# Gathered rows turned by a 16-bit DMA transpose instead of by TensorE

## The chip, the cores and the metric

One core of one Trainium2 chip runs the whole program. The metric is the device time of one execution in microseconds (us), as the median of several runs. The core has five engines with a queue of instructions each: TensorE (PE; its weight loads are listed apart as PEld), VectorE (DVE), ScalarE (ACT), GpSimd (POOL) and SyncE (SP). SP only issues DMAs; GpSimd issues the indirect ones.

## The reference

A gated linear attention (batch 4, 8 heads, 768 positions, head size 48) keeps a 48 x 48 state per head; its output is viewed as 3072 tokens of 384 numbers. A noisy gate picks 2 of 8 experts for each token; each expert is a two-layer network (384 to 1024 to 384, relu). A dense two-layer network follows (384 to 2048 to 384, leaky). All numbers are float32.

```python
state = alpha_t[:, None] * state + outer(k_t, v_t);  y_t = q_t @ state
noisy = x @ w_gate + log1p(exp(x @ w_noise)) * noise       # top 2 of 8, softmax of the two
out[token] += weight * (relu(x[token] @ w1[e]) @ w2[e])
h = out @ w_in;  result = maximum(0.01 * h, h) @ w_out
```

## The kernel before, in words

**Stages.** The attention works through 24 units of 128 tokens. Each unit ends with a turn of its output to rows of tokens (`turn_y`), a copy out of PSUM by ScalarE (`copy_x`, L1026) and a store to the DRAM buffer `x_d` (L1033). Routing gives each choice of a token a slot in `idx_d` (scatter by GpSimd, L1142). Then 16 expert groups follow, two per expert: group kind 0 has 384 slots (3 blocks of 128 rows), kind 1 has 480 (4 blocks of 120). The first two groups, experts 0 and 1 with kind 0, take rows of the first 2048 tokens alone and so can begin early. Eight dense groups of 384 tokens end the program.

**Input of a group.** For each block `gather1` (L511) fetches rows of `x_d` by an indirect DMA into the tile `xg` (a ring of six). `turn` (L521 to L529) turns the block with three 128-column transposes on TensorE into the PSUM tile `pA` (a ring of two). `turned_hi` (L533, ScalarE) copies the result rounded into `xh`, and `turned_lo` (L538, VectorE) stores the rest into `xl`; there are two sets of `xh` and `xl`. For a dense group `gather2` (L731) fetches the two experts' rows of each token, and `combine` (L738 on ScalarE, L740 on VectorE) adds them by weight; the result is turned in the same way.

**Products.** `gemm1` (L669) does nine matmuls for 128 hidden columns, three pieces of 128 rows with three products of halves of precision, into `ph` (two PSUM buffers). `hidden` makes `hh` (L686, ScalarE) and `hl` (L693, VectorE) out of it, in dense groups by way of `hc` (L679 to L696). `gemm2` (L708) does three matmuls per block and step into `py`, two steps behind `gemm1`. A group has 8 such steps, a dense group 16. `rows_out` and `rows_stored` (L725) bring the result to `y_d` or to the output.

**Order.** A planner written in Python (`Planner`) places every step: it is given the engine (p, a, v, g, s, or a choice such as vg), an estimated duration, an extra latency for DMAs (`lat`), the steps that it depends on, the rings that it takes and a due time. It always takes the step that can start earliest by its own estimates, and among equals the one due first. The result is a fixed order on each engine; the chip then waits by semaphores. The SP queue carries, in that order, loads of attention inputs, weights (`fetch`, L444, L447), stores of `x_d` and `y_d`, and the spills and reloads of the dense weights (L482, L487).

```python
w = add("p", 0.34, lambda j=j: turn(key, j), own + AUX.get((key, j), []), ...,
        due=tm[0] - 7 + 0.8 * j if phase == 2 else 1e9)
hi = add("a", 0.5, lambda j=j: turned_hi(key, j), ...)
lo = add("v", 0.57, lambda j=j: turned_lo(key, j), [hi], ...)
```

Of the kernel before, what the change touches and what calls it, by code (L numbers as in the profile page):

```python
# [7 lines left out]
FT = mybir.dt.float32  # L8
# [3 lines left out]
U32 = mybir.dt.uint32  # L12
AF = mybir.ActivationFunctionType
# [15 lines left out]
F64B = 2  # L29
XGB = 6  # L30
# [293 lines left out]
def tile_kernel(  # L324
# [39 lines left out]
    x_d = dram.tile([N, Dm], FT, name="x_d")  # L364
# [130 lines left out]
    def slots_of(t, g):  # L495
        return t[1 + E * OFF[g]:1 + E * (OFF[g] + GR[g]), :].rearrange("(p j e) d -> p j e d", e=E, j=len(GB[g]))

    def rows_of(t, e, g, j):

        return slots_of(t, g)[:, j, e, :]  # L500
# [3 lines left out]
    def load_idx(i, g):  # L504
        src = slots_of(idx_d, g).rearrange("p j e o -> p (j e o)")
        nc.sync.dma_start(idx_sb[i][:GB[g][0][1]].rearrange("p j e -> p (j e)"), src.bitcast(U32))

    def gather1(e, g, j, rows, i):
        o, n = GB[g][j]
        xg = xgp.tile([128, Dm], FT, name="xg")  # L510
# [8 lines left out]
    XT, XP = {}, {}  # L519

    def turn(key, j):  # L521
        if j == 0:
            pool = pools["M" if len(XT) % 2 else "E"]
            XT[key] = [pool.tile([128, KD, GMAX], FR, name=nm, bufs=1) for nm in ("xh", "xl")]
        o, n = blocks(key)[j]
        src = xg_t.pop(key + (j,))
# [4 lines left out]
    def turned_hi(key, j):  # L531
        o, n = blocks(key)[j]
        nc.scalar.activation(XT[key][0][:, :, o:o + n], XP[key, j][:, :, :n], AF.Copy)  # L533
# [44 lines left out]
    def build_experts(t0, R, stored, scat, early_in, ready_at, totals, acc_done, begun):  # L578
# [7 lines left out]
        def rows_in(e, g):  # L586
            for j in range(len(GB[g])):
                if g == 0 and e < EARLY:
                    deps, rows = [early_in] + stored[:EARLY_TILES * NG], EARLY_TILES * TT
                else:  # L590
                    deps, rows = [late_in[1 - g]] + stored, N
                GX["a", e, g, j] = add("g", 1.29, lambda j=j, rows=rows: gather1(e, g, j, rows, 2 if rows < N else g), deps, takes=[R["xg"]],
                                       lat=2.0)

        def turned(key, phase):
            done = []
            for j, (o, n) in enumerate(blocks(key)):
                own = [XO[key]] if j else []
                w = add("p", 0.34, lambda j=j: turn(key, j), own + AUX.get((key, j), []),
                        use=[(GX[key + (j,)], R["xg"])] + [(x, R["XT"]) for x in own],  # L600
                        takes=[R["pA"]] + ([] if j else [R["XT"]]), phase=phase, due=tm[0] - 7 + 0.8 * j if phase == 2 else 1e9)
                if not j:
                    XO[key] = w
                hi = add("a", 0.5, lambda j=j: turned_hi(key, j), use=[(w, R["pA"]), (XO[key], R["XT"])], phase=phase)
                lo = add("v", 0.57, lambda j=j: turned_lo(key, j), [hi], use=[(w, R["pA"]), (XO[key], R["XT"])], phase=phase)
                done += [hi, lo]
            return done
# [126 lines left out]
        def combine(g, j, kk):  # L734
            c = g * (GROUP2 // 128) + j
            ya = YG["b", g, j, 0]
            if kk == 0:
                nc.scalar.activation(ya, ya, AF.Copy, scale=wts[:, c, 0:1])  # L738
            else:
                nc.vector.scalar_tensor_tensor(ya, YG["b", g, j, 1], wts[:, c, 1:2], ya, op0=OP.mult, op1=OP.add)  # L740
                xg_t["b", 0, g, j] = ya
# [5 lines left out]
        def group_in(gi):  # L747
# [3 lines left out]
            else:  # L751
                for j in range(len(blocks(key))):
# [6 lines left out]
                    GX[key + (j,)] = ga  # L759
                    AUX[key, j] = [cb]  # L760
                    ga.holders[R["xg"]].append(cb)
# [69 lines left out]
    with ExitStack() as actx:  # L831
# [14 lines left out]
            scr=1, pend=PB, pA=2, xg=XGB, XT=2, W=NA + NB, w1s=2, w2s=2, ph=2, hh=4, hl=4, py=4, ys=3, hc=2, f64=F64B, f64o=2).items()}  # L846
# [6 lines left out]
        def build_unit(u):  # L853
# [178 lines left out]
            cx = add("a", 0.5, copy_x, use=[(ty, R["pA"])], takes=[R["x"]])  # L1032
            xo = add("s", 0.07, lambda: nc.sync.dma_start(x_d[u * C:(u + 1) * C, :], d["x"].rearrange("p h s d -> p (h s d)")),  # L1033
# [177 lines left out]
    with tc.If(fv > 0):  # L1211
        general(tc, dict(q=q, k=k, v=v, alpha=alpha), identf, hm, desc, wgn_l, noise, x_d, w1, w2, w_in, w_out, out)
# [219 lines left out]
```

## Time and profile before

| what | value |
|---|---|
| median of 3 runs | 1102.26 us (1102.2 to 1102.77) |
| span of the profiled execution | 1088.6 us |
| median less that span | 13.7 us |
| mean granted TensorE clock | 0.987 |
| instructions in the span | 17738 |
| DMA traffic | 127.37 MB, 117 GB/s in the mean |

The span runs from the first to the last instruction of one execution. The profile gives no total for that execution beside its span, so the span is set against the median of the runs. Each engine's busy time is a sum over its instructions; matmuls are pipelined, so that the records of neighbours overlap, and a granted clock of 1.0 is 2.4 GHz. In a timeline a line gives the start, the time, the engine, the source line, the operation with its result and inputs, and how many were merged, and in brackets the idle time before it and who ended it.

### The profile page before, as it was taken

What the parts mean: (1) busy time and instruction counts of PE and PEld (TensorE: products, weight loads), DVE (VectorE), ACT (ScalarE), POOL (GpSimd) and SP (SyncE); (2) the same over time, 40 slices, a digit from 0 to 9 for tenths busy, and PEclk for the clock granted to TensorE, in tenths of its full rate; (3) what the DMA queues carried; (4) which work ended last, traced back from release to release, by engine and by line L of the source; (5) the groups of instructions that cost most, each with busy time, mean ns of one, the idle gap of its engine ahead of it and who ended that gap; (6) DMA issues with size and microseconds to landing.
All of it is one profiled execution on the core that took longest, in us unless ns stands there. A gap on an engine that the chain in (4) does not pass through costs nothing.

```text
span 1088.6 us, 17738 instructions
## 1 busy us (share of the span) xinstructions
PE 1056.3 (97%) x6600; PEld 989.9 (91%) x6600; DVE 585.1 (54%) x1199; ACT 392.2 (36%) x835; POOL 325.3 (30%) x386
## 2 busy tenths in 40 slices
PE   7989897999999999999999999999999999999997
PEld 5756763999999999999999999999999999999997
DVE  8797964522545564654565334555554545454543
ACT  5656554322444453534453333231222222222211
POOL 4456676531123343544262131310110102010000
PEclk9998998999999999999999999999999999999999
DMA  9989813133544464655476665320101111000000
GB/s 253 287 177 224 162 56 122 26 92 108 157 120 162 145 211 134 215 162 162 156 230 213 193 202 169 116 66 9 58 19 48 30 37 34 32 23 23 1 22 26
DMA packets 76967, 127.37 MB, mean 117 GB/s; under 512 B 10407, under 2 KB 54311, under 8 KB 76871
## 3 DMA queue, kind: packets, MB, share of 16 engines
q1 hardware_dynamic: 68679, 106.05, 33.0%
q0 software_dynamic: 8192, 20.09, 6.6%
q8 instruction: 54, 0.88, 0.4%
q14 instruction: 42, 0.34, 0.1%
HBM read 93.42 MB, written 32.69 MB: 116 GB/s over the span
## 4 chain that ended last, share of the span: by engine, by line
PE 82%; issue 0%; DVE 0%; ACT 0%; DMA 0%; ACTq 0%
PE py L708 40%; PE ph L669 39%; PE pA L529 2%; DVE w1lB L457 0%; ACT ys L718 0%; DVE w2lB L457 0%; ACT w1hB L453 0%; DVE xl L538 0%; PE pA L557 0%; DVE g_um L201 0%; DVE g_u L193 0%; DMA x_d<-x 0%; ACTq L453 0%; PE pA L1113 0%; ACTq L718 0%
## 5 line engine op out<-in xcount | busy, mean ns | idle before, releaser
L693 DVE SCALAR_TENSOR_TENSOR hl<-ph,hh 128x384 fp32r<-128x384 f32 (+1 forms) x128 | 77.5, 606 | 200.3 <-ACT hh L686 200.3
L679 ACT ACTIVATE hc<-ph 128x384 f32<-128x384 f32 x128 | 62.9, 492 | 294.9 <-PE ph L669 294.9
L682 DVE SCALAR_TENSOR_TENSOR hc<-hc 128x384 f32<-128x384 f32 x128 | 71.5, 558 | 174.7 <-ACT hc L679 174.7
L686 ACT ACTIVATE hh<-ph 128x384 fp32r<-128x384 f32 (+1 forms) x128 | 68.0, 532 | 259.2 <-PE ph L669 247.7
L708 PE MATMUL py<-w2hA,hh 128*128 128x384 f32 (+1 forms) x416 | 142.1, 342 | 0.0
L708 PE MATMUL py<-w2hB,hh 128*128 128x384 f32 (+1 forms) x416 | 141.6, 340 | 0.0
L708 PE MATMUL py<-w2hA,hl 128*128 128x384 f32 (+1 forms) x416 | 140.5, 338 | 0.0
L708 PE MATMUL py<-w2lA,hh 128*128 128x384 f32 (+1 forms) x416 | 140.2, 337 | 0.0
L708 PE MATMUL py<-w2lB,hh 128*128 128x384 f32 (+1 forms) x416 | 140.0, 337 | 0.0
L708 PE MATMUL py<-w2hB,hl 128*128 128x384 f32 (+1 forms) x416 | 140.0, 337 | 0.0
L669 PE MATMUL ph<-xh,w1hA 128*128 128x384 f32 (+1 forms) x384 | 136.0, 354 | 0.0
L669 PE MATMUL ph<-xl,w1hA 128*128 128x384 f32 (+1 forms) x384 | 134.2, 350 | 0.0
L669 PE MATMUL ph<-xh,w1lA 128*128 128x384 f32 (+1 forms) x384 | 133.9, 349 | 0.0
L669 PE MATMUL ph<-xh,w1hB 128*128 128x384 f32 (+1 forms) x384 | 133.9, 349 | 0.0
L669 PE MATMUL ph<-xl,w1hB 128*128 128x384 f32 (+1 forms) x384 | 133.6, 348 | 0.0
L669 PE MATMUL ph<-xh,w1lB 128*128 128x384 f32 (+1 forms) x384 | 133.5, 348 | 0.0
L731 POOL DMA_INDIRECT xg<-y_d,gidx x48 | 48.7, 1015 | 263.2 <-PE pA L529 212.5
L511 POOL DMA_INDIRECT xg<-x_d,idx x56 | 55.5, 991 | 106.1 <-PE pA L529 83.3
L708 PEld LDWEIGHTS py<-w2lB,hh 128*128 128x128 f32 (+1 forms) x416 | 77.3, 186 | 1.0
L708 PEld LDWEIGHTS py<-w2lA,hh 128*128 128x128 f32 (+1 forms) x416 | 77.3, 186 | 0.9
L708 PEld LDWEIGHTS py<-w2hA,hh 128*128 128x128 f32 (+1 forms) x416 | 77.3, 186 | 0.8
L708 PEld LDWEIGHTS py<-w2hB,hh 128*128 128x128 f32 (+1 forms) x416 | 77.3, 186 | 0.8
(153 smaller groups left out, 1942.9 us busy)
## 6 DMA issues: line engine op xcount, KB each, us to landing
w1s<-in_moe_w_dram SPq DMA_DIRECT2D x32, 384.0 KB, 4.3
w2s<-in_moe_w_dram SPq DMA_DIRECT2D x32, 384.0 KB, 3.9
kq<-in_kq_l_dram SPq DMA_DIRECT2D x24, 448.0 KB, 6.3
nv<-in_v_l_dram SPq DMA_DIRECT2D x24, 256.0 KB, 6.1
w1s<-in_moe_w_in_dram SPq DMA_DIRECT2D x24, 256.0 KB, 3.9
w2s<-in_moe_w_out_dram SPq DMA_DIRECT2D x16, 384.0 KB, 3.9
y_d<-ys SPq DMA_DIRECT2D x32, 180.0 KB, 2.4
at<-in_al_l_dram SPq DMA_DIRECT2D x24, 226.2 KB, 5.9
```

Of the source, the lines that this page charges most:

```text
L511: nc.gpsimd.indirect_dma_start(out=xg[:n, :], out_offset=None, in_=x_d[0:rows, :], in_offset=bass.IndirectOffsetOnAxis(ap=idx_sb[i][:n, j, ...
L529: nc.tensor.transpose(p[:, d, :n], src[:n, d * 128:(d + 1) * 128], identf[:n, :n])
L669: nc.tensor.matmul(ps[:, :n], a[:, d, fo:fo + 128], x[:, d, :n], start=i == 0, stop=i == len(seq) - 1)
L679: nc.scalar.activation(hc[:, :n], ps[:, :n], AF.Copy)
L682: nc.vector.scalar_tensor_tensor(hc[:, :n], hc[:, :n], 0.01, hc[:, :n], op0=OP.mult, op1=OP.max)
L686: nc.scalar.activation(hh[:, :n], ps[:, :n], AF.Relu)
L693: nc.vector.scalar_tensor_tensor(hl[:, :n], ps[:, :n], 0.0, hh[:, :n].bitcast(FT), op0=OP.max, op1=OP.subtract)
L708: nc.tensor.matmul(py[:n, :], h[:, o:o + n], w[:, f % 2, :], start=(f == 0 and i == 0), stop=(f == nf - 1 and i == 2))
L731: nc.gpsimd.indirect_dma_start(out=yg, out_offset=None, in_=y_d[0:rows, :], in_offset=bass.IndirectOffsetOnAxis(ap=gidx[:, c, kk:kk + 1], ...
```

## The change

The attention output is stored as two planes of 16-bit halves, first the 384 high halves of a row and then the 384 low ones. A gathered block is then 128 rows of 768 halves. SP issues a DMA that transposes it from SBUF to SBUF into the tile `xb` (`cross`). Two copies, each by VectorE or GpSimd as the planner chooses, put the high and the low halves back side by side into the float32 tile `xi` (`join`). `turned_hi` and `turned_lo` read `xi` in SBUF instead of `pA` in PSUM. In dense groups one more copy by GpSimd takes the combined rows apart into planes first (`part`). Rings of two are added for `xb`, `xi` and `yp`. Blocks are now full ones of 128 with a rest, so kind 1 has 128, 128, 128 and 96 rows, and slots run block by block instead of interleaved; the index load of kind 1 is two DMAs. The planner's due time of the transpose is 2 us earlier than that of the turn was.

```diff
 def blocks_of(n):
-    nb = -(-n // 128)
-    assert n % nb == 0
-    return [(j * (n // nb), n // nb) for j in range(nb)]
+    assert n % 16 == 0
+    return [(o, min(128, n - o)) for o in range(0, n, 128)]
+def planes(t):
+    return t.rearrange("p (w d) -> p w d", w=2)
+def words(t):
+    return t.bitcast(U16).rearrange("p (d w) -> p w d", w=2)
...
-    x_d = dram.tile([N, Dm], FT, name="x_d")
+    x_d = dram.tile([N, 2 * Dm], U16, name="x_d")
...
     def load_idx(i, g):
-        src = slots_of(idx_d, g).rearrange("p j e o -> p (j e o)")
-        nc.sync.dma_start(idx_sb[i][:GB[g][0][1]].rearrange("p j e -> p (j e)"), src.bitcast(U32))
+        nf = GR[g] // 128
+        parts = [(0, nf)] + ([(nf, 1)] if GR[g] % 128 else [])
+        for j, nj in parts:
+            src = slots_of(idx_d, g, j, nj).rearrange("p j e o -> p j (e o)")
+            nc.sync.dma_start(idx_sb[i][:GB[g][j][1], j:j + nj, :], src.bitcast(U32))
...
-    def turn(key, j):
...
-        p = XP[key, j] = ps2.tile([128, KD, 128], FT, name="pA")
-        for d in range(KD):
-            nc.tensor.transpose(p[:, d, :n], src[:n, d * 128:(d + 1) * 128], identf[:n, :n])
+    def cross(key, j):
+        o, n = blocks(key)[j]
+        src = xg_t.pop(key + (j,))
+        t = XB[key, j] = xgp.tile([128, 2, KD, 128], U16, name="xb", bufs=2)
+        nc.sync.dma_start_transpose(t.rearrange("p w d n -> p (w d) n")[:, :, :n], src[:n, :])
+    def join(key, j, w, en):
+        o, n = blocks(key)[j]
+        if w == 0:
+            XP[key, j] = xgp.tile([128, KD, 128], FT, name="xi", bufs=2)
+        dst = XP[key, j].bitcast(U16).rearrange("p d (n w) -> p d n w", w=2)[:, :, :n, 1 - w]
+        (nc.vector if en == "v" else nc.gpsimd).tensor_copy(dst, XB[key, j][:, w, :, :n])
...
-                own = [XO[key]] if j else []
-                w = add("p", 0.34, lambda j=j: turn(key, j), own + AUX.get((key, j), []),
-                        use=[(GX[key + (j,)], R["xg"])] + [(x, R["XT"]) for x in own],
-                        takes=[R["pA"]] + ([] if j else [R["XT"]]), phase=phase, due=tm[0] - 7 + 0.8 * j if phase == 2 else 1e9)
+                own, ring = GX[key + (j,)]
+                x = add("s", 0.07, lambda j=j: cross(key, j), AUX.get((key, j), []), use=[(own, ring)], takes=[R["xb"]],
+                        lat=3.0, phase=phase, due=tm[0] - 9 + 0.8 * j if phase == 2 else 1e9)
+                w0 = add("vg", dict(v=0.5, g=0.8), lambda en, j=j: join(key, j, 0, en), use=[(x, R["xb"])], takes=[R["xi"]],
+                         phase=phase)
+                w1 = add("vg", dict(v=0.5, g=0.8), lambda en, j=j: join(key, j, 1, en), [w0],
+                         use=[(x, R["xb"]), (w0, R["xi"])], phase=phase)
...
+        def part(g, j):
+            yp = xg_t["b", 0, g, j] = pools["M"].tile([128, 2 * Dm], U16, name="yp", bufs=2)
+            nc.gpsimd.tensor_copy(planes(yp), words(YG["b", g, j, 0])[:, ::-1, :])
...
             def copy_x():
-                d["x"] = work.tile([128, HP, 2, D], FT, name="x", bufs=3)
-                nc.scalar.activation(d["x"], d["px"].rearrange("p h (s d) -> p h s d", s=2)[:, :, :, 0:D], AF.Copy)
+                d["x"] = work.tile([128, 2 * Dm], U16, name="x", bufs=3)
+                src = d["px"].rearrange("p h c -> p (h c)").bitcast(U16).rearrange("p (h d w) -> p w h d", h=H, w=2)
+                nc.scalar.activation(planes(d["x"]).rearrange("p w (h d) -> p w h d", h=H), src[:, ::-1, :, 0:D], AF.Copy)
...
-            cx = add("a", 0.5, copy_x, use=[(ty, R["pA"])], takes=[R["x"]])
+            cx = add("a", 0.85, copy_x, use=[(ty, R["pA"])], takes=[R["x"]])
```

## Rows read from the trace of the kernel before

**Rows 1.** The page, busy time of each engine, its share and instructions.
```profile
PE 1056.3 (97%) x6600; PEld 989.9 (91%) x6600; DVE 585.1 (54%) x1199; ACT 392.2 (36%) x835; POOL 325.3 (30%) x386
```

**Rows 2.** The chain of waits, share of the span by line.
```profile
by line: PE py L708 40.1%; PE ph L669 39.5%; PE pA L529 2.4%; issue 0.3%; DVE w1lB L457 0.2%; ACT ys L718 0.1%; DVE w2lB L457 0.1%; ACT w1hB L453 0.1%; DVE xl L538 0.0%; PE pA L557 0.0%; DVE g_um L201 0.0%; DVE g_u L193 0.0%; DMA x_d<-x 0.0
```

**Rows 3.** Stretches: us, busy time (instructions) of each engine, TensorE clock, DMA share, GB/s.
```profile
0.00:180.00 180.00, 160.75 (x1554) 115.86 (x1554) 138.08 (x316) 100.25 (x232) 106.49 (x175) 0.96 0.73 181
...
181.70:189.40 7.70, 2.92 (x13) 1.99 (x13) 4.93 (x11) 4.74 (x11) 6.18 (x6) 0.58 0.72 208
...
240.94:668.30 427.36, 427.36 (x2362) 408.40 (x2361) 210.27 (x388) 174.52 (x361) 141.49 (x138) 1.00 0.54 169
668.30:1088.60 420.30, 413.69 (x2384) 412.87 (x2383) 209.94 (x426) 96.50 (x198) 42.99 (x42) 0.99 0.13 41
```

**Rows 4.** Line L529 alone: instructions, ns min/median/max, first and last start.
```profile
L529 PE MATMUL pA<-identf,xg x240: 263/271/476, 181.8 to 1018.6; 128*128 128x128 f32 x72, 120*128 120x120 f32 x48
```

**Rows 5.** Timeline of TensorE at two turned blocks: start us, us, what.
```profile
546.01 0.49 PE L529 MATMUL pA<-identf,xg 128*128 128x128 f32 x3
...
546.87 0.49 PE L529 MATMUL pA<-identf,xg 128*128 128x128 f32 x3
```

**Rows 6.** Chain of waits in the first group, and two groups of instructions by shape.
```profile
198.48 1.58 PE ph L669 x9
...
L686 ACT ACTIVATE hh<-ph 128x384 fp32r<-128x384 f32 x64 | 31.5, 492 | 113.7 <-PE ph L669 110.8 <-PE pA L1114 2.7
...
L693 DVE SCALAR_TENSOR_TENSOR hl<-ph,hh 128x384 fp32r<-128x384 f32 x64 | 35.6, 556 | 91.7 <-ACT hh L686 91.7
```

**Rows 7.** Entrance: timelines of GpSimd and TensorE, then the chain of waits.
```profile
178.52 1.00 POOL L511 DMA_INDIRECT xg<-x_d,idx  x1 [6.51 <-DMA idx<-idx_d]
...
181.09 0.95 POOL L511 DMA_INDIRECT xg<-x_d,idx  x1 [0.30 <-issue]
...
181.75 0.52 PE L529 MATMUL pA<-identf,xg 128*128 128x128 f32 x3 [1.78 <-DMA xg<-x_d,idx]
...
187.88 1.54 PE L529 MATMUL pA<-identf,xg 128*128 128x128 f32 x6 [3.58 <-DVE xl L538]
...
189.42 3.46 PE ph L669 x9
```

**Rows 8.** DMA issues, us to landing (median); then two lines' min/median/max, L511, L487.
```profile
out_dram<-ys SPq DMA_DIRECT2D x24, 192.0 KB, 1.9
...
xg<-x_d,idx POOLq DMA_INDIRECT x56, 3.3
...
DMA to landing us min/median/max: 3.0/3.3/6.2
...
DMA to landing us min/median/max: 3.5/4.9/8.2
```

**Rows 9.** Groups of instructions by shape: busy us, mean ns; idle before.
```profile
L688 DVE CAST hh<-hc 128x384 fp32r<-128x384 f32 x128 | 46.1, 360 | 12.1 <-PE py L708 0.9
...
L538 DVE TENSOR_TENSOR xl<-pA,xh 128x384 fp32r<-128x384 f32 x48 | 25.6, 553 | 11.0 <-ACT xh L533 10.7
...
L453 ACT ACTIVATE w1hB<-w1s 128x768 fp32r<-128x768 f32 x16 | 13.5, 842 | 4.2 <-issue 3.3 <-DMA w1s<-in_moe_w_dram 0.9
...
L1026 ACT ACTIVATE x<-pA 128x384 f32<-128x384 f32 x24 | 11.8, 490 | 3.6 <-PE pA L1022 2.9 <-ACT pos L1118 0.7
...
L457 POOL TENSOR_TENSOR w1lB<-w1s,w1hB 128x768 fp32r<-128x768 f32 x5 | 9.4, 1889 | 29.6 <-ACT w1hB L453 29.5
```

**Rows 10.** Timelines of VectorE and TensorE before the first dense group.
```profile
662.84 0.61 DVE L740 SCALAR_TENSOR_TENSOR xg<-xg,wts 128x384 f32<-128x384 f32 x1
...
668.48 0.33 PE L669 MATMUL ph<-xh,w1hB 128*128 128x384 f32 x1
```

**Rows 11.** Timeline of TensorE: the third group's last turn and first product.
```profile
232.59 0.47 PE L529 MATMUL pA<-identf,xg 120*128 120x120 f32 x3
...
240.78 0.37 PE L669 MATMUL ph<-xh,w1hA 128*128 128x480 f32 x1
```

More of the change, by code (lines that the diff above doesn't have):

```diff
@@ L12 @@
 U32 = mybir.dt.uint32
+U16 = mybir.dt.uint16
 AF = mybir.ActivationFunctionType
@@ L493, in tile_kernel, with slots_of @@
     xg_t = {}
-    def slots_of(t, g):
-        return t[1 + E * OFF[g]:1 + E * (OFF[g] + GR[g]), :].rearrange("(p j e) d -> p j e d", e=E, j=len(GB[g]))
+    def slots_of(t, g, j, nj=1):
+        o, n = GB[g][j]
+        return t[1 + E * (OFF[g] + o):1 + E * (OFF[g] + o + n * nj), :].rearrange("(j p e) d -> p j e d", e=E, j=nj)
     def rows_of(t, e, g, j):
-        return slots_of(t, g)[:, j, e, :]
+        return slots_of(t, g, j)[:, 0, e, :]
     idx_sb = [consts.tile([128, len(GB[g]), E], U32, name=f"idx{i}") for i, g in enumerate((0, 1, 0))]
     def load_idx(i, g):
-        src = slots_of(idx_d, g).rearrange("p j e o -> p (j e o)")
-        nc.sync.dma_start(idx_sb[i][:GB[g][0][1]].rearrange("p j e -> p (j e)"), src.bitcast(U32))
+        nf = GR[g] // 128
[3 more added lines that the diff above has]
+            nc.sync.dma_start(idx_sb[i][:GB[g][j][1], j:j + nj, :], src.bitcast(U32))
     def gather1(e, g, j, rows, i):
         o, n = GB[g][j]
-        xg = xgp.tile([128, Dm], FT, name="xg")
+        xg = xgp.tile([128, 2 * Dm], U16, name="xg")
         nc.gpsimd.indirect_dma_start(out=xg[:n, :], out_offset=None, in_=x_d[0:rows, :],
@@ L518, in tile_kernel, with turned_hi @@
     GMAX = max(G0, G1, GROUP2)
-    XT, XP = {}, {}
-    def turn(key, j):
+    XT, XB, XP = {}, {}, {}
+    def cross(key, j):
[9 more added lines that the diff above has]
+        (nc.vector if en == "v" else nc.gpsimd).tensor_copy(dst, XB[key, j][:, w, :, :n])
+    def turned_hi(key, j):
+        o, n = blocks(key)[j]
         if j == 0:
@@ L592, in rows_in @@
                 GX["a", e, g, j] = add("g", 1.29, lambda j=j, rows=rows: gather1(e, g, j, rows, 2 if rows < N else g), deps, takes=[R["xg"]],
-                                       lat=2.0)
+                                       lat=2.0), R["xg"]
         def turned(key, phase):
@@ L597, in turned @@
             for j, (o, n) in enumerate(blocks(key)):
-                own = [XO[key]] if j else []
-                w = add("p", 0.34, lambda j=j: turn(key, j), own + AUX.get((key, j), []),
-                        use=[(GX[key + (j,)], R["xg"])] + [(x, R["XT"]) for x in own],
-                        takes=[R["pA"]] + ([] if j else [R["XT"]]), phase=phase, due=tm[0] - 7 + 0.8 * j if phase == 2 else 1e9)
+                own, ring = GX[key + (j,)]
[5 more added lines that the diff above has]
+                         use=[(x, R["xb"]), (w0, R["xi"])], phase=phase)
+                hi = add("a", 0.5, lambda j=j: turned_hi(key, j), [w1],
+                         use=[(w0, R["xi"])] + ([(XO[key], R["XT"])] if j else []), takes=[] if j else [R["XT"]], phase=phase)
                 if not j:
-                    XO[key] = w
-                hi = add("a", 0.5, lambda j=j: turned_hi(key, j), use=[(w, R["pA"]), (XO[key], R["XT"])], phase=phase)
-                lo = add("v", 0.57, lambda j=j: turned_lo(key, j), [hi], use=[(w, R["pA"]), (XO[key], R["XT"])], phase=phase)
+                    XO[key] = hi
+                lo = add("v", 0.57, lambda j=j: turned_lo(key, j), [hi, w1], use=[(w0, R["xi"]), (XO[key], R["XT"])], phase=phase)
                 done += [hi, lo]
@@ L758, in group_in @@
                     cb = add("v", 0.64, lambda j=j: combine(key[2], j, 1), [ca], use=[(ga, R["xg"]), (gb, R["xg"])], phase=2)
-                    GX[key + (j,)] = ga
-                    AUX[key, j] = [cb]
-                    ga.holders[R["xg"]].append(cb)
+                    pt = add("g", 1.5, lambda j=j: part(key[2], j), [cb], use=[(ga, R["xg"])], takes=[R["yp"]], phase=2)
+                    GX[key + (j,)] = pt, R["yp"]
             xdone[gi] = turned(key, 1 if gi == 0 else 2)
@@ L1031, in build_unit @@
             ty = add("p", 0.46, turn_y, [cy], use=[(xs[T][0], R["xt"])], takes=[R["pA"]], due=b + PERIOD + 8)
-            cx = add("a", 0.5, copy_x, use=[(ty, R["pA"])], takes=[R["x"]])
-            xo = add("s", 0.07, lambda: nc.sync.dma_start(x_d[u * C:(u + 1) * C, :], d["x"].rearrange("p h s d -> p (h s d)")),
+            cx = add("a", 0.85, copy_x, use=[(ty, R["pA"])], takes=[R["x"]])
+            xo = add("s", 0.07, lambda: nc.sync.dma_start(x_d[u * C:(u + 1) * C, :], d["x"]),
                      use=[(cx, R["x"])], size=0.2)
@@ L1211, in tile_kernel @@
     with tc.If(fv > 0):
-        general(tc, dict(q=q, k=k, v=v, alpha=alpha), identf, hm, desc, wgn_l, noise, x_d, w1, w2, w_in, w_out, out)
+        general(tc, dict(q=q, k=k, v=v, alpha=alpha), identf, hm, desc, wgn_l, noise, x_g, w1, w2, w_in, w_out, out)
 def general(tc, src, identf, hm, desc, wgn_l, noise, x_d, w1, w2, w_in, w_out, out):
```

8 lines of the change are left out of this document (2 added, 6 removed).

## The prediction

> **What bounds the kernel now.** I read the busy times first, then the chain of waits, then the stretches. TensorE is busy 97% of the span, VectorE 54%, ScalarE 36% and GpSimd 30% [rows 1]. The chain that ended last lies on matmuls for 82%: 40.1% in the second product (L708), 39.5% in the first (L669) and 2.4% in the turning of gathered rows (L529), which is 26.1 us [rows 2]. The stretches say where this holds. In the first 180 us (linear attention and routing) TensorE is busy 160.75 us and VectorE 138.08 us, so several engines share that bound. From 181.70 to 189.40 us TensorE works only 2.92 us of 7.70 at a granted clock of 0.58: this is the entrance to the experts. From 240.94 to 668.30 us it is never idle, and to the end it misses 6.6 us [rows 3]. So, from the entrance on, what is taken off TensorE is taken off the time, as long as nothing else comes late.
>
> **What is removed.** 240 transposes at L529, three to a block, so 80 blocks [rows 4]. Two neighbouring blocks start 0.86 us apart with three matmuls of L708 between them [rows 5]; nine matmuls of a step take 1.58 us, 0.176 each [rows 6], so a block costs 0.86 - 0.53 = 0.335 us. All 80 come to 26.8 us, near the chain's 26.1. Four of them ran in the gap before 189.42 us [rows 7] and return nothing: 76 x 0.335 = **-25.5 us**.
>
> **What is added: the DMA transpose.** Its time T from issue to landing is shown nowhere here; a block is 128 x 768 halves, 192 KB. From below: a store of 192 KB by the same queue lands in 1.9 us. From above: the longest landing of a reload is 8.2 us. The nearest row is the gather, with the same bytes as 128 rows into SBUF, 3.3 us in the median and 6.2 at most [rows 8]. I take T = 3.5 us and keep 1.9 to 8.2 for the range. The Trainium skill, page "DMA: Bandwidth & Descriptors", section "Latency and other measured facts", gives 261 GB/s for a transposing DMA; by an estimate from that page the bytes would take 0.75 us and T would stay near the gather's, so the sum by it is the same.
>
> **The two joins, high and low of a block** are copies of 384 halves: a VectorE copy of 384 elements takes 0.36 us [rows 9]. A strided 2-byte write could be quicker or slower; I take 0.45 and bound it by 0.2 and by GpSimd's 1.9 for 768 elements. 160 of them are 72 us, on engines that are about half idle; they cost time only where the chain is bare. The high copy by ScalarE and the low subtraction by VectorE stay as they are, 0.49 and 0.55 us.
>
> **The entrance** is bare. Gathers go out at 178.52 us and every 1.28 us; the first turn waited for its data until 181.75 [rows 7]. Now: first transpose 181.8 to 185.3, two joins to 186.2; there are two buffers, so the third transpose issues only then and lands at 189.8, joins to 190.7, high and low copies to 191.8, and with handovers and the splits of weights on the same two engines the first product begins near 192.4 instead of 189.42: **+3 us**. It moves by 2 us for each us of T: 0 at T = 2, +12.4 at 8.2. The first nine matmuls took 3.46 us instead of 1.58, behind an engine that had idled [rows 6, 7]. A longer idle may prolong the low clock: **+1**, bounds -1.9 (clock back by then) to +5.
>
> **Attention.** The copy of the attention output now writes 768 halves in two planes. ScalarE takes 0.49 us for 384 elements and 0.84 for 768 [rows 9], so 24 x 0.35 = 8.4 us more. ScalarE is idle for 80 of these 180 us [rows 3], and the copy feeds only a store and the freeing of a PSUM buffer. **+1**, bounds 0 and 8.4.
>
> **The first dense group.** Each of the 24 dense blocks gets one more copy on GpSimd (768 halves, 1 to 1.9 us). GpSimd works 43 us of the last 420 [rows 3], and a group lasts some 50 us, so seven groups hide it. Before the first, the last combine starts at 662.84 and the first product at 668.48 [rows 10]: 5.6 us, against 0.6 + 1.5 + 3.5 + 0.9 + 1.0 = 7.5 us now, less what TensorE can fill with the second products still open: **+1**, bounds 0 and +5.
>
> **What is moved, and costed at nothing.** SP gets 80 issues that wait at its head for a gather and for a free buffer; behind them stand fetches of weights, stores, spills and reloads. A group's input can be made one whole group (25 us and more) ahead, since two sets of it exist, and that hides them; without that cover each late block would cost its lateness. The index load is now cut into shorter runs and for the second kind of group into two DMAs; in the third group turning ended 8 us before its first product [rows 11], which covers one landing more. Blocks of 128, 128, 128 and 96 instead of four of 120 leave the number and width of the matmuls alone.
>
> **Sum.** -25.5 + 3 + 1 + 1 + 1 = -19.5 us. The profiled span is 1088.6 us; the median of the runs is 1102.26, so 13.7 us lie around the span, which I leave unchanged: span 1069, time **1083 us**.
>
> **Rivals.** First, the entrance is free: T near 2, clock and attention unharmed. For it speaks the 1.9 us store, against it that a transpose reads and writes in smaller pieces than a row. 1102.3 - 25.5 = 1077.
> Second, a dear entrance: T = 6 gives +8 there, +3 at the third group, +1.9 for the clock, +3 at the first dense group and +3 in attention; -25.5 + 18.9, 1096. For it: single gathers took 6.2 us.
> Third, **slower**: late transposes hold VectorE's queue. The order was written with 3.07 us for the transpose, and a join whose data is late blocks the low half of the hidden rows (L693) behind it, which frees the PSUM buffer of the first product. From the end of a first product to the reuse of its buffer lie three pieces of 1.58 us; ScalarE and VectorE take 0.49 + 0.56 of it [rows 6, 9], so about 3.5 us are spare and harm begins at T = 6.6. Two pairs of blocks in each of 22 groups then cost 44 x (T - 6.6). It turns the sum's sign at T = 6.9; at 8.2 it is 44 x 1.6 = 70, the entrance 12.4 and the rest 3, so 1102.3 + 60 = 1162. For it: weights share the queue, and a reload did take 8.2 us. Against it: later blocks gain on TensorE once it has been held, so the stalls need not all add up.
> The Trainium skill, page "VectorE: DVE Perf Modes", section "The three transpose paths", speaks against this change: 1.309 us by DMA for 128 x 128 of two bytes against 0.39 by TensorE, and TensorE where PSUM will do. By an estimate from it, six such squares one after another make T 7.9 and the time 1149 us; no run here shows a DMA transpose.
> That TensorE keeps the work is excluded by the diff.
>
> **Chances.** Forecast 52% (its own range 1076 to 1092), free entrance 13%, dear entrance 17%, slower 18%. The measurement tells about 0.2% (2.2 us) from no change. Faster: 52 + 13 + 13 of the dear entrance's 17 = 78%; the same: the other 4%; slower 18%. The range runs from T near 2 with the clock back early (1075) to just under the old time (1100), which leaves out the slower case and little below.
>
> **What would show it.** L529 gone from TensorE; transposes on SP's queue landing in 3 to 4 us; the first L669 near 192 us of the span; no idle TensorE from 240 us on except a us or so before the first dense group; VectorE some 50 to 70 us busier; the attention copy at 0.85 us. Wrong, if transposes land in 7 us or more, if L693 or L669 wait for joins group after group, or if SP's queue makes weights late.

## The result, and the profile after

The changed kernel takes **1114.9 us** (median of 4 runs, 1109.8 to 1118.15) where the kernel before takes 1102.23 beside it: a ratio of 1.0107, 95% interval 1.009 to 1.0125. It is 12.7 us slower; 1083 had been forecast.

The unchanged kernel takes 1090 us beside some of the experiments below and 1100 to 1102 beside the others, so each time is read against the kernel before measured beside it, and the trace of the changed kernel (span 1110.4) against a later trace of the unchanged one from where it takes 1100 (label e12_before_again, span 1098.0) and not against the first one (1088.6). The two spans differ by 12.4 us, as the times do.

The stretches of e12_before_again, cut at the last store of rows, at the first product of the experts and at the first product of the dense groups; columns as in [rows 3]:

```profile
0.00:190.70 190.70, 164.07 (x1554) 117.96 (x1554) 136.90 (x317) 100.31 (x233) 107.19 (x175) 0.92 0.69 171
190.70:199.50 8.80, 2.54 (x13) 1.79 (x13) 5.34 (x13) 4.78 (x12) 6.97 (x7) 0.72 0.71 215
199.50:677.78 478.28, 478.28 (x2654) 458.70 (x2654) 230.06 (x444) 189.93 (x393) 168.64 (x164) 1.00 0.51 159
677.78:1098.00 420.22, 413.49 (x2383) 412.66 (x2381) 210.08 (x426) 96.49 (x198) 43.58 (x42) 1.00 0.13 40
```

The same stretches of the changed kernel:

```profile
0.00:196.40 196.40, 162.12 (x1545) 120.34 (x1546) 135.88 (x318) 106.87 (x232) 103.71 (x173) 0.90 0.61 166
196.40:214.17 17.77, 3.06 (x11) 0.71 (x8) 9.43 (x24) 8.40 (x16) 11.38 (x10) 0.70 0.91 211
214.17:697.39 483.22, 464.98 (x2503) 444.01 (x2503) 266.16 (x480) 191.72 (x395) 202.51 (x216) 0.98 0.63 178
697.39:1110.40 413.01, 406.58 (x2304) 405.58 (x2304) 239.39 (x454) 95.56 (x196) 89.53 (x94) 0.99 0.19 50
```

The attention is 5.7 us longer (196.4 against 190.7), the entrance 9.0 (17.8 against 8.8), the experts 4.9 (483.2 against 478.3), and the dense part 7.2 shorter. In the experts TensorE's busy time fell from 478.28 to 464.98, as it should without the turning, but it now stands idle for 18.2 us where it was never idle: 13.9 of them before the first dense product, 2.1 behind the first product and 2.2 at 275.8 us. The next lines are the busy times of the page and the turning by lines, the answers to [rows 1, 4, 9]: transposes on SP's queue, and the joins on GpSimd and VectorE.

```profile
PE 1036.7 (93%) x6360; PEld 970.6 (87%) x6360; DVE 650.9 (59%) x1273; ACT 402.5 (36%) x838; POOL 407.1 (37%) x493
...
L538 SPq DMA_TRANSPOSE xb<-xg x56: 1196/1214/2852, 198.4 to 597.1; - x56
...
L545 POOL COPY xi<-xb x86: 513/692/1323, 212.8 to 1000.6; 128x384 uint16<-128x384 uint16 x77, 128x288 uint16<-128x288 uint16 x9
L545 DVE COPY xi<-xb x74: 366/392/2643, 203.6 to 950.9; 128x384 uint16<-128x384 uint16 x67, 128x288 uint16<-128x288 uint16 x7
```

The lines give ns as min/median/max. In the median each price is near its estimate: a join 0.39 us on VectorE (0.45 assumed), 0.69 on GpSimd, the wide copy 0.81 (0.84). In the mean a full join takes 0.60 us on VectorE and 0.77 on GpSimd, and all joins together 105.6 us where 72 were assumed. That is spread over two engines that are busy 59% and 37% of the span, so the loss must lie in where the work stands in the order. The entrance, for [rows 7]: first a line of SP's queue and two of VectorE, then the chain of waits (start us, us, what):

```profile
198.41 1.32 SPq L538 DMA_TRANSPOSE xb<-xg  x1
...
203.64 0.38 DVE L545 COPY xi<-xb 128x384 uint16<-128x384 uint16 x1
...
212.72 0.38 DVE L545 COPY xi<-xb 128x384 uint16<-128x384 uint16 x1 [3.44 <-DMA xb<-xg]
```

```profile
201.56 4.92 DMA xb<-xg
...
207.35 8.29 DMA xb<-xg
...
215.66 0.38 DVE xi L545
216.04 0.83 DVE xl L557
...
216.92 1.33 PE ph L692 x3
```

The first block's transpose is issued at 198.41 us; its joins, behind the splits of weights on VectorE (L466), run from 203.64 to 204.40. That frees a buffer: the third block's transpose is issued at 204.98 and joined from 212.72, 7.7 us later, and the first product follows at 214.17. The chain of waits leads on to the second matmul, which waits 2.06 us more for the low copy xl; on VectorE the join of the next group's first block stands ahead of it, whose transpose took 8.29 us. The chain before the first dense product, for [rows 10]:

```profile
671.53 1.00 DVE f64f L322
...
672.67 0.09 POOL f64g L326
...
673.55 1.01 POOL xg L754
...
678.62 4.85 DMA xg<-y_d,gidx
683.48 0.62 DVE xg L763
...
684.14 0.88 POOL yp L767
...
696.81 0.53 ACT xh L552
...
697.39 0.69 PE ph L692
```

From the last expert product to the dense one there is first a piece of work on the dense weights (the f64 names: splitting their 64-bit words, spread over VectorE, ScalarE and GpSimd), then the gathers behind it on GpSimd, then the new copies. TensorE waited 13.9 us (683.45 to 697.39).

### The profile page after: what moved, and what is told of

Its sections match the earlier page's. It is cut to its first block, busy times and chain, and to the rows that moved or that the text cites. A ratio compares the mean times of both kernels' runs of the same rounds, so it can differ in the third digit from the quotient of the medians.

```text
span 1110.4 us, 17619 instructions
## 1 busy us (share of the span) xinstructions
PE 1036.7 (93%) x6360; PEld 970.6 (87%) x6360; DVE 650.9 (59%) x1273; ACT 402.5 (36%) x838; POOL 407.1 (37%) x493
## 2 busy tenths in 40 slices
DMA packets 140224, 142.70 MB, mean 129 GB/s; under 512 B 73696, under 2 KB 117600, under 8 KB 140128
## 3 DMA queue, kind: packets, MB, share of 16 engines
q1 hardware_dynamic: 132064, 121.40, 39.8%
## 4 chain that ended last, share of the span: by engine, by line
PE 87%; DVE 4%; DMA 3%; another core or an unknown queue 2%; ACT 2%; issue 1%; POOL 1%; SPq 0%; DVEq 0%; ACTq 0%; POOLq 0%
PE ph L692 38%; PE py L731 38%; PE pS L969 2%; PE pY L1022 2%; DMA xb<-xg 2%; PE pM L1001 1%; PE pA L1076 1%; PE pY L1028 1%; PE pA L1047 1%; PE pM L956 1%; PE pM L1005 1%; DMA xg<-y_d,gidx 1%; DMA at<-in_al_l_dram 1%; DVE xi L545 1%
## 5 line engine op out<-in xcount | busy, mean ns | idle before, releaser
L545 POOL COPY xi<-xb 128x384 uint16<-128x384 uint16 (+1 forms) x86 | 62.2, 751 | 286.9 <-DVE xl L557 253.2
L705 DVE SCALAR_TENSOR_TENSOR hc<-hc 128x384 f32<-128x384 f32 x128 | 76.4, 597 | 136.3 <-ACT hc L702 132.6
L692 PE MATMUL ph<-xh,w1hB 128*128 128x384 f32 (+1 forms) x384 | 134.2, 350 | 13.9 <-ACT xh L552 13.9
L692 PE MATMUL ph<-xh,w1hA 128*128 128x384 f32 (+1 forms) x384 | 134.6, 351 | 11.7 <-ACT xh L552 11.7
L692 PE MATMUL ph<-xl,w1hA 128*128 128x384 f32 (+1 forms) x384 | 134.6, 351 | 2.1 <-DVE xl L557 2.1
L692 PE MATMUL ph<-xl,w1hB 128*128 128x384 f32 (+1 forms) x384 | 134.5, 350 | 0.0
L692 PE MATMUL ph<-xh,w1lB 128*128 128x384 f32 (+1 forms) x384 | 134.1, 349 | 0.0
L692 PE MATMUL ph<-xh,w1lA 128*128 128x384 f32 (+1 forms) x384 | 134.0, 349 | 0.0
L692 PEld LDWEIGHTS ph<-xh,w1hB 128*128 128x128 f32 x384 | 72.8, 190 | 16.4 <-ACT xh L552 14.3
L692 PEld LDWEIGHTS ph<-xh,w1hA 128*128 128x128 f32 x384 | 72.7, 189 | 14.2 <-ACT xh L552 11.8
L719 DVE TENSOR_TENSOR hl<-hc,hh 128x384 fp32r<-128x384 f32 x128 | 76.6, 598 | 10.1
L731 PEld LDWEIGHTS py<-w2hA,hl 128*128 128x128 f32 (+1 forms) x416 | 77.3, 186 | 3.0 <-DVE hl L716 2.6
L524 POOL DMA_INDIRECT xg<-x_d,idx x56 | 59.2, 1057 | 54.9 <-DMA xb<-xg 24.0
```

The costliest lines, as they stand in the source:

```text
L545: (nc.vector if en == "v" else nc.gpsimd).tensor_copy(dst, XB[key, j][:, w, :, :n])
L692: nc.tensor.matmul(ps[:, :n], a[:, d, fo:fo + 128], x[:, d, :n], start=i == 0, stop=i == len(seq) - 1)
L705: nc.vector.scalar_tensor_tensor(hc[:, :n], hc[:, :n], 0.01, hc[:, :n], op0=OP.mult, op1=OP.max)
L719: nc.vector.tensor_sub(hl[:, :n], HT[si, "hc"][:, :n], hh[:, :n].bitcast(FT))
L731: nc.tensor.matmul(py[:n, :], h[:, o:o + n], w[:, f % 2, :], start=(f == 0 and i == 0), stop=(f == nf - 1 and i == 2))
```

## The experiments

All times are against the kernel before beside them; a ratio has its 95% interval. Line numbers differ between the kernels: the first product is L669 in the kernel before, L692 in the changed one and L720 in those of experiments 6 to 9 and 11 that turn some groups by TensorE. The cuts of code leave out lines that carry no argument (...).

**1. The attention copy alone.** Kernel before, with the wide copy; TensorE still turns the rows. Both planes get the high halves, the low ones are left out.

```
+ d["x"] = work.tile([128, 2 * Dm], U16, name="x", bufs=3)
+ nc.scalar.activation(planes(d["x"])..., src[:, 1:2, :, 0:D].to_broadcast([128, 2, H, D]), AF.Copy)
...
- cx = add("a", 0.5, copy_x, ...)
+ cx = add("a", 0.85, copy_x, ...)
```

> The kernel before, with one part of the change: copy_x writes 768 halves and the planner is told 0.85 us for it; TensorE still turns the rows, through a view of the row as 384 words. Both planes are filled with the high halves, so the turned rows are not the reference's values; the amount of work is that of the kernel before. In the two traces the attention ended 16.2 us later after the change (180.2 and 196.4 us). Theory A, the wider copy or the order the planner makes with its price costs the attention that much: 1110 to 1118 us, last store of x_d near 190 to 196 us. Theory B, the late end came from something else (the stretches of 4 to 8 us in which ScalarE waited for work that the trace could not name): 1100 to 1106 us, last store near 180 to 184 us.

Measured: 1093.83 against 1090.02 us, 1.0031 (1.002 to 1.0043). The expectations of experiments 1, 2, 3 and 7 were set from a kernel before of 1102 us, so they are read as differences: +3.8 us is at the upper end of theory B's (-2 to +4). The last store of x_d, at 177.6 us, is not late at all; the first product is, at 193.4 instead of 189.4.

**2. The same copy, order as before** (the planner's 0.5 left alone).

> As the run before it, but the planner is still told 0.5 us for copy_x, so that the order of every engine is that of the kernel before and only the copy's real length changes (0.49 us to about 0.81, 24 of them, 7.7 us of ScalarE). Both planes again hold the high halves, so the turned rows are not the reference's values. Theory A1, ScalarE's extra time is on the attention's path: 1106 to 1112 us, near the run with 0.85. Theory A2, the loss is the planner's new order: 1101 to 1104 us, while the run with 0.85 stands at 1110 or more. Theory B: both within 1100 to 1106 us.

Measured: 1089.95 us, 0.9997 (0.9987 to 1.0006), with the copy at 0.81 us. What follows: the copy's length costs nothing that can be told from the noise, as ScalarE has room; the planner's new order, made from its price, costs 3.9 us, and costs it at the entrance. This part of theory A holds, though it had expected 8 to 16.

**3. All but the attention part.** ScalarE writes 384 values rounded to 16 bits, and the store puts them into both planes; the low halves are left out.

```
- d["x"] = work.tile([128, 2 * Dm], U16, name="x", bufs=3)
+ d["x"] = work.tile([128, Dm], BF, name="x", bufs=3)
...
- cx = add("a", 0.85, copy_x, ...)
+ cx = add("a", 0.5, copy_x, ...)
...
+ dma_start(planes(x_d[...]), d["x"].bitcast(U16)[:, None, :].to_broadcast([128, 2, Dm]))
```

> The kernel after, without its attention part: copy_x writes 384 values rounded to bfloat16 in 0.5 us, as long as before, and the store puts them into both planes, so the bytes of x_d, the gathers, the DMA transposes and the joins are those of the kernel after. The turned rows are a rounding of the reference's, with the high half repeated below. If the attention part costs the 16 us that its later end suggests (theory A), the rest of the change is worth what is left: 1098 to 1104 us. If the late end of the attention has another cause, such as a disturbance that belongs to DMA transposes or scatters (theory B): 1110 to 1116 us.

Measured: 1094.11 us, 1.0032 (1.0017 to 1.0048): +4.1 us, between theory A (-4 to +2) and theory B (+8 to +14), and nearer to A. Even without its attention part the change is a loss. The experts begin 7.5 us late (196.9 us), and the wait before the dense group is 13.6 us again.

**4. The changed kernel again, and with the old price.** The second tells the planner 0.5 us for the wide copy.

> The kernel after, unchanged, beside the kernel before on this chip, on which before takes 1090 us. If the two parts measured here add up (the attention's order 3.8 us, the rest 4.1 us) and the unnamed waits of 4 to 8 us in the attention of the first trace were a disturbance of that execution: 1096 to 1100 us, with the last store of x_d near 182 to 190 us. If those waits belong to the kernel: 1102 to 1108 us, and they stand in this trace too, in the stretches with eight scatters in a row.

> The kernel after, but the planner is told 0.5 us for the wide copy_x instead of 0.85, so that the attention keeps the order of the kernel before. If the attention part is its order alone, this is as fast as the run whose attention was as before: 1092 to 1096 us. If the wide copy's length counts once the rows are turned by DMA, it stands with the kernel after, 1097 us or more.

Measured: 1097.2 against 1090.18 us, 1.0062 (1.0049 to 1.0076), and 1094.53, 1.0044 (1.0029 to 1.0058). Here the change costs 7.0 us, and 2.7 less with the old price (the runs of the second spread over 6 us). The stretch from the last store of x_d to the first product, in e5_after_again and then in e6_after_old_plan:

```profile
182.35:201.68 19.33, 4.62 (x12) 0.96 (x11) 9.01 (x21) 8.37 (x16) 10.93 (x11) 0.68 0.90 194
...
181.18:195.60 14.42, 1.19 (x6) 0.50 (x4) 6.22 (x11) 6.45 (x14) 6.75 (x8) 0.66 0.69 161
```

In the first trace of the kernel before it is 9.2 us (180.23 to 189.42). So with the old price the entrance grows by 5.2 us instead of 10.1: about half of its growth comes with the planner's order. The long waits without a name, of 4 us and more, are gone.

**5. The kernel before, traced again.**

> The kernel before, unchanged, for its trace on this chip. Its time was 1102 us beside two sets of runs and 1090 beside two others. If the chips differ in one stage: on a chip of 1102 us the first product of the first group begins near 200 us instead of 189.4 and the rest of the span is 899 us as in the first trace; on a chip of 1090 us it repeats the first trace. If the chips differ evenly in everything, the part behind the first product is 908 us on a chip of 1102.

Measured: 1100.47 us, 0.9998 (0.9987 to 1.001). First product at 199.5 us, the rest 898.5 us (899.2 in the first trace): the two traces differ in the attention alone, by 10 us. ScalarE's lines, of this trace and then of the changed kernel's:

```profile
154.80 0.60 ACT L948 ACTIVATE ar<-pS 128x512 f32<-128x512 f32 x1 [5.26 <-remote]
...
118.23 0.60 ACT L1042 ACTIVATE xt<-pY 128x512 f32<-128x512 f32 x1 [8.01 <-remote]
```

"remote" is a release that no record of the profile names. Every trace taken where the kernel before takes 1100 us or more has two or more such waits of 3.8 to 8 us on ScalarE in the attention, this one 3.82 and 5.26; no trace taken where it takes 1090 has one, and neither has the first trace. So they are no part of the change. What they wait for is open, and that they make up the whole 10 us is not shown. The changed kernel's attention is 5.7 us later than here, not the 16 us by which it trails the first trace; but its trace has 8.01, 4.88 and 4.17 us of such waits, 8 us more than this one, and in experiment 4, without them, its last store is 2.1 us late (182.35 against 180.23). The 5.7 us are therefore not shown to be the change's.

**6. The dense groups alone.** From the second dense group on, DMA transposes; all else TensorE.

```
+ BY_PE = set(groups[:2 * E + 1])
...
+ if key in BY_PE:
+     w = add("p", 0.34, lambda j=j: turn(key, j), ...)
```

> Attention, x_d, the sixteen expert groups and the first dense group as before, turned by TensorE; only the 21 blocks of dense groups 2 to 8 go through the part copy, the DMA transpose and the joins. If the steady part simply loses 0.335 us per block and nothing is late there: 1090 - 7 = 1083 us (1081 to 1085), no idle time of TensorE behind the first dense group. If the DMA transposes or their copies make the dense weights' last pieces late (as where both kinds of group were turned by DMA, 9.3 us before the third step of the dense part): 1088 us or more.

Measured: **1083.53 us, 0.9932** (0.9918 to 0.9945). Its stretches:

```profile
189.20:668.50 479.30, 479.30 (x2654) 457.63 (x2654) 231.27 (x444) 190.01 (x393) 166.77 (x164) 1.00 0.51 158
668.50:1081.80 413.30, 406.69 (x2320) 406.30 (x2319) 234.75 (x446) 95.13 (x193) 84.21 (x90) 0.99 0.19 51
```

Up to the dense part nothing changes; from there 6.8 us are gone, 21 blocks of 0.32 us. Where the transposes are covered the working of the prediction holds.

**7. A mixture: both entrances by TensorE.** Attention and x_d as before; the first group and the first dense group by TensorE; the other 74 blocks by DMA.

```
+ BY_PE = {groups[0], groups[2 * E]}
...
+ nc.gpsimd.tensor_copy(planes(yp[:n, :]), words(src[:n, :])[:, ::-1, :])
```

> A mixture. Attention, x_d and gathers as before the change; the first group and the first dense group are turned by TensorE as before; the other 74 blocks by DMA transposes, the expert groups' rows parted into planes by a copy of GpSimd (as the change does for the dense groups). Theory 1, the steady part gains 0.335 us per block and the losses lie in the attention and the two bare entrances: 1102.2 - 74 x 0.335 = 1077.4, with a few us for new waits 1077 to 1085 us. Theory 2, DMA transposes cost the steady part too (late blocks, VectorE or ScalarE delayed): 1092 us or more.

Measured: 1095.88 us, 1.0063 (1.0044 to 1.0082). Theory 1 (a gain of 17 to 25 us) failed although both entrances were whole again (first product at 187.5 us, first dense one at 659.2); the time is theory 2's. The loss had moved on:

```profile
721.93 0.66 PE L720 MATMUL ph<-xh,w1hA 128*128 128x384 f32 x1 [9.25 <-DMA w1hA<-w_d]
```

The dense weights are split in 40 pieces and spilled; the first split starts near 330 us, and the last spill came at 715 us, 667 before. Besides the 9.25 us TensorE waited 5.3 us in five smaller pieces between 701 and 730 us. The pieces run through VectorE and GpSimd, where the plane copies and joins now stand too, and are fetched through SP's queue, where the transposes stand; which of these queues delays them most was not separated.

**8. The copies on other engines.** The plane copies on ScalarE, all joins on VectorE.

```
- nc.gpsimd.tensor_copy(planes(yp[:n, :]), words(src[:n, :])[:, ::-1, :])
+ nc.scalar.activation(planes(yp[:n, :]), words(src[:n, :])[:, ::-1, :], AF.Copy)
...
- w0 = add("vg", dict(v=0.5, g=0.8), ...)
+ w0 = add("v", 0.4, ...)
```

> The mixture again, with the plane copies of the gathered rows on ScalarE (planned 0.85 us) instead of GpSimd and all joins on VectorE (planned 0.4), so that GpSimd has no more work than before the change. If GpSimd's load made the dense weights' spills late (last one at 715 us, 667 before): last spill by 690 us, the wait of 9.3 us before the dense weights gone and 1074 to 1084 us. If VectorE's joins or the number of queue steps is what delays them: the wait stays, 1090 us or more.

Measured: 1092.63 us, 1.0016 (1.0 to 1.0031); last spill at 704, and TensorE still waited, 4.05 us for w1lA and 6.31 for the hidden rows' copy hc. Also, in the first group it waited 3.81 us for hl (L744), held on VectorE behind a join of the second group whose transpose was late: the prediction's third rival, once. The theory failed: GpSimd's load alone is not the cause. VectorE's load rose in the same edit.

**9. The dense weights begun earlier.** One edit, made in the mixture and in the changed kernel (with 0.5 us told for the copy):

```
- [S1[first[2 * EARLY]]["g1"]], takes=[R[nm]], ...
+ [S1[first[1]]["g1"]], takes=[R[nm]], ...
```

> The first mixture (first group and first dense group by TensorE, 74 blocks by DMA, plane copies on GpSimd), with one edit: the splitting of the dense weights may begin behind the first step of the second group (near 215 us) instead of the fifth group (near 305 us). Theory: the copies slow the 40 pieces of the dense weights, whose last spill came at 715 us instead of 667, and TensorE waited 9.3 us for the reload. With 90 us more lead the wait goes: 1078 to 1084 us, no idle time over 2 us behind 660 us. Rival: the dense start is held by VectorE itself (it was busy 8.0 of 8.0 us from 700 to 708), and then 1088 to 1094 us.

> The kernel after with 0.5 us told for copy_x, and the dense weights' splitting begun near 215 us instead of 305. It asks what makes the idle time of 13.6 us before the first dense product. Theory 1, GpSimd's pieces of the dense weights stand ahead of the gathers of the first dense group (gathers went out at 658 us, 13 us later than before the change): the gathers go out near 645 us, the idle time falls to 6 us or less, 1085 to 1089 us. Theory 2, it is the order on ScalarE and VectorE (the combine stands behind the last expert group's output copies) and the longer chain of part, transpose, joins and split: the idle time stays 11 to 14 us, 1091 to 1096 us.

Measured: the mixture **1085.51 against 1102.29 us, 0.9847** (0.9833 to 0.986); the changed kernel 1095.73, 0.9953 (0.9935 to 0.9971). The mixture gains 16.8 us, more than the 6 to 12 that its theory gave against 1090; no wait behind 660 us is over 1.1 us. The second's 6.6 us under the kernel before are theory 1's (1 to 5 under 1090) and a little more; the wait it asks about is gone. GpSimd ahead of the first dense group, in the changed kernel:

```profile
671.51 0.73 POOL L325 TENSOR_TENSOR f64g<-f64g,f64e 128x256 f32<-128x256 f32 x1 [4.19 <-ACT f64h L318]
672.67 0.74 POOL L326 TENSOR_TENSOR f64g<-f64f,f64g 128x256 fp32r<-128x256 f32 x1 [0.42 <-DVE f64f L322]
673.55 1.01 POOL L754 DMA_INDIRECT xg<-y_d,gidx  x1
```

and with the early splitting, e10_after_early64, with TensorE's first dense product:

```profile
653.38 1.02 POOL L754 DMA_INDIRECT xg<-y_d,gidx  x1 [34.24 <-DMA y_d<-ys]
...
680.72 0.44 PE L692 MATMUL ph<-xh,w1hB 128*128 128x384 f32 x1 [0.47 <-ACT xh L552]
```

There the last spill comes at 616 us instead of 726. The gathers wait for their rows alone, and TensorE waits 0.47 us instead of 13.9: in this order the wait hung on the late pieces of the dense weights.

**10. The weight fetches moved from the entrance.** The changed kernel, 0.5 us told, and

```
  group_in(0)
+ for i in range(NP, 2 * NP):
+     expert_weights(i, begun(i) + xdone[0])
```

> The kernel after with 0.5 us told for copy_x, and the second expert's weights fetched only when the first group's rows are split, so that no weight fetch stands in the queue beside the first three DMA transposes. Theory 1, a transpose's 3.8 to 8 us at the entrance come from the fetches that share the queue: joins start within 2.5 to 3 us of the issue, and the first product comes near 190 to 192 us instead of 195.6. Theory 2, they come from the transposes and joins themselves: the first product stays at 194 to 197 us. The whole time says less here, since the second expert's weights can then come late for the second group.

Measured: 1108.97 us, 1.0067 (1.0051 to 1.0083); the first product stands 12.8 us behind the last store of rows, 15.3 in e10_after_early64, beside the same kernel before. SP's queue, then VectorE's joins, of this run:

```profile
194.14 3.02 SPq L538 DMA_TRANSPOSE xb<-xg  x2
197.26 0.52 SPq L1061 DMA_DIRECT2D x_d<-x  x1
201.20 10.94 SPq L538 DMA_TRANSPOSE xb<-xg  x4
```

```profile
200.51 0.66 DVE L545 COPY xi<-xb 128x384 uint16<-128x384 uint16 x2 [10.81 <-issue]
203.60 0.68 DVE L545 COPY xi<-xb 128x384 uint16<-128x384 uint16 x2 [2.43 <-issue]
208.72 0.39 DVE L545 COPY xi<-xb 128x384 uint16<-128x384 uint16 x1 [3.17 <-issue]
```

With no weight fetch in the queue the first block's join begins 6.4 us after the issue (194.14 to 200.51), and the third block's transpose goes out only when the first block is joined (201.20), its own join 7.5 us later. The fetches are worth at most the 2.4 us. Theory 1 failed and theory 2 stands as far as it goes: gathers and scatters run at the same time, and whether they slow the transposes was not tried.

**11. The mixture repeated, and with its first dense group by DMA.** The second has BY_PE = {groups[0]}.

> The mixture with the early splitting of the dense weights, unchanged: it stood at 0.985 of the kernel before on a chip of 1102 us. If its gain lies behind the first product (18.7 us against the first trace), it is 15 to 19 us faster than before on any chip: 1072 to 1075 us where before takes 1090.

> The same mixture, but the first dense group too is turned by DMA transposes; only the first group is left to TensorE. If the wait before the first dense group came from the late splitting of the dense weights alone, it does not come back, and the time is 1 us below to 2 us above the mixture. If the longer chain of part, transpose, joins and split is itself bare there: 5 to 13 us above the mixture, with idle time of TensorE before the first dense product.

Measured: 1085.88 against 1100.99 us, 0.9849 (0.9828 to 0.987), and 1093.33, 0.9917 (0.9893 to 0.994). The gain of the mixture repeats. Turning the first dense group by DMA costs 7.5 us more, with 7.8 us of idle time, though the splitting was begun as early as in the mixture. SP's queue there:

```profile
663.93 1.34 SPq L543 DMA_TRANSPOSE xb<-yp  x1
669.73 1.44 SPq L776 DMA_DIRECT2D y_d<-ys  x3
671.26 0.41 SPq L490 DMA_DIRECT2D w_d<-f64g  x1
671.76 1.22 SPq L543 DMA_TRANSPOSE xb<-yp  x1
```

The second block's transpose stands behind three stores of the last expert group, which can only go when TensorE has ended that group. The last spills, at 692 us (688 in the mixture), still run beside it, and one of them (L490) stands ahead of the transpose too. So the late pieces are not the only way to lose here: a transpose is exposed wherever the order puts it behind an output of the work that it was to run beside. In e10_after_early64 the order happened to avoid it: all three transposes of the group are issued before those stores (672.73 and 679.24 us).

The best version is that of 9: its stretches from the last store of rows on, in e13_mixed_again, beside those of the two kernels above.

```profile
192.60:200.74 8.14, 2.67 (x10) 1.52 (x10) 5.31 (x11) 4.86 (x13) 6.44 (x6) 0.54 0.73 216
200.74:673.20 472.46, 468.14 (x2512) 447.14 (x2512) 272.99 (x497) 193.93 (x399) 244.80 (x254) 0.99 0.68 182
673.20:1084.70 411.50, 404.22 (x2304) 403.66 (x2303) 235.34 (x455) 95.47 (x195) 86.45 (x92) 1.00 0.19 51
```

The entrance is back at 8.1 us, the experts are 5.8 us and the dense part 8.7 us shorter than in e12_before_again. The gain is 15.1 us of the 23.7 that 74 blocks of 0.32 us would give.

## Why the prediction was wrong

**What is removed: right.** From the first product of the fifth group to that of the twelfth (25 blocks) e12_before_again takes 206.3 us and the changed kernel 198.3: 0.32 us a block, 0.335 forecast. Experiment 6 shows the gain by itself.

**The transpose and the joins: right in the middle, wrong at the tail.** T was taken as 3.5 us; landings of L538 in e5_after_again:

```profile
DMA to landing us min/median/max: 2.7/3.7/7.8
```

By the estimate from the Trainium skill, "VectorE: DVE Perf Modes", section "The three transpose paths", T would be 7.9 us. The median disagrees with that; the longest agrees. The third rival, VectorE's queue held group after group from T = 6.6 on, was not seen: T reached that at the entrance and in single blocks elsewhere (6.6 and 7.1 us at most), and TensorE's waits for hl came to 0.8 to 5 us in a whole kernel, 2.2 in the changed one.

**The entrance: the step that failed first.** "+3 us" took T = 3.5 us, near the median of all blocks, for the blocks of the entrance, and the order as unchanged. The entrance grew by 9.0 us. The landings up to 200 us in e5_after_again and up to 190 us in e6_after_old_plan:

```profile
DMA to landing us min/median/max: 5.8/6.8/7.8
...
DMA to landing us min/median/max: 3.9/4.9/5.8
```

By the prediction's own rule, 2 us for each us of T, these medians give +9.6 and +5.8; the two entrances grew by 10.1 and 5.2. So the mechanism, two transposes in series because of two buffers, was right, and T at this place was the term mis-sized; the planner's order, which is all that differs between the two kernels, moved it. That the rule fits this well is partly luck: in the changed kernel the first block's joins also stood behind weight splits (6.0 us from issue to their end, 4.4 forecast), and the steps behind the third block took 1.5 us instead of 2.6. What makes T long here is open (experiment 10). The second rival had T = 6 and +8 here and, with its other parts, 1096 us; its step for this place was the nearer one. The +1 for a longer low clock held: the first matmuls behind the entrance run at half the clock, which costs 2.1 us here and 1.2 in e12_before_again.

**Attention: +1, measured +3.8 alone.** The mechanism named was ScalarE's time, which costs nothing (experiment 2). That the planner orders all engines anew when a price in it changes was not a term of the sum, and what it costs falls on the entrance. Its sign was not to be foreseen; the bounds, 0 and 8.4, were made for the other mechanism and held it by luck.

**The first dense group: the second failed step.** "+1, bounds 0 and +5", measured 13.9 us of idle time. GpSimd's 43 us were read from the stretch behind 668 us, but what feeds this group runs ahead of it, where GpSimd finishes the dense weights. With the new transposes and copies those 40 pieces end 49 us later (last spill 726 instead of 677), and in order behind them stood the gathers. Begun 90 us earlier, the pieces no longer hold this group (experiment 9). The wait has a second price that no term had: the clock falls to half during it, and the first 14 matmuls of the dense part take 4.6 us instead of 2.5. The joins were costed at nothing "on engines that are about half idle"; the cover was there for the joins, but not for the longest chain of small steps that shared their queues.

**The sum.** On paper -25.5 + 6; in the spans +5.7 (attention), +9.0 (entrance), +4.9 (experts) and -7.2 (dense) make +12.4. The last two close with the price of a block: the experts lose 55 blocks of 0.32 us (-17.6) and gain 18.2 of idle time, 1.0 of low clock and 2.8 of second products of the last expert group that ran behind the first dense product before and now run ahead of it (1344 of them in this stretch instead of 1329); the dense part loses 21 blocks (-6.7) and these 2.8, and gains 2.1 of low clock. The attention's 5.7 are not shown to be the change's (experiment 5); beside the kernel before of 1090 us the change costs 7.0 us and not 12.7. The 13.7 us "around the span" were none: a run's time is 1.7 us above its span (1099.71 and 1098.0 in e12_before_again). Trace and median did not belong together, so the step from span to time was unsound, though it only carried the difference over.

**What stays open:** what ScalarE's unnamed waits in the attention are, what slows the transposes of the entrance when no weight fetch is beside them, and which queue makes the pieces of the dense weights late.

## What to carry to other kernels

Moving work off a full engine pays where the new path is covered by other work: turn the blocks of the bare entrances where they were turned, and only the others elsewhere. Before costing small copies at nothing on half-idle engines, look for the longest chain of small steps that shares their in-order queues, and ask who waits for its end; here one edit that let that chain begin 90 us earlier turned +0.6% into -1.5% for the same copies (where the kernel before takes 1090 and where it takes 1102 us). Where a planner writes the order, a changed price is a change of its own: test it apart.

## What the runs showed of the hardware

A DMA transpose of 128 x 768 halves holds SP's queue 1.21 us in the median at each issue (the rows for L538), so 80 of them take 97 us of it; a plain store of x_d took 0.33. It moves in small pieces: packets under 512 B rise from 10,407 to 73,696, 60,032 of them of 256 B, and the queue's share of the DMA engines from 33.0% to 39.8%:

```profile
DMA packets 140224, 142.70 MB, mean 129 GB/s; under 512 B 73696, under 2 KB 117600, under 8 KB 140128
...
q1 hardware_dynamic: 132064, 121.40, 39.8%
```

A copy of 384 halves into every second 16-bit place takes VectorE 0.38 us in the median, no longer than one of 384 words ([rows 9] 0.36), as long as GpSimd computes nothing beside it: 33 of the 67 full joins in the changed kernel, the longest 0.56. The 34 that overlap an instruction of GpSimd take 0.81 in the median and up to 2.64. In e8_mixed_act, where GpSimd has no copies, 114 of 132 run alone at 0.38. So two half-idle engines were not independent here; what it cost was not tried apart.
